# Attention and two expert layers: scores, exponentials and maxima in single PSUM banks, two of each, and four instead of seven of nine key tiles in full float32 in the first batch

## The chip, the cores and the metric

The kernel runs on one core of one Trainium2 chip. The metric is the device time of one execution in microseconds (us), here the median of three. Engines are named as in the profile: PE is TensorE (matmuls; PEld its weight loads), DVE is VectorE, ACT is ScalarE, POOL is GpSimd, SP is SyncE, which issues most of the DMAs.

## What is computed

Attention with pooled queries over 4 batches of 8 heads, then a dense layer of three products with a maximum, then a layer of 8 experts with one expert for each token. Only the first part is touched by the change.

```python
q_pool = q.reshape(B, H, S // factor, factor, D).mean(axis=3)     # 4, 8, 576, 64
scores = scale * np.matmul(q_pool, k.transpose(0, 1, 3, 2))       # 576 x 1152 a head
scores = scores - np.max(scores, axis=-1, keepdims=True)
attn = np.exp(scores)
attn = attn / (np.sum(attn, axis=-1, keepdims=True) + 1e-09)
x = np.matmul(attn, v)                                            # 576 x 64 a head
...
h = np.maximum(np.maximum(x @ w1, x @ w2), x @ w3)                # 2304 x 512 -> 768
x = h @ w_out                                                     # -> 512
...
e_idx = np.argmax(x @ w_gate, axis=1)                             # one of 8 experts
ye = np.maximum(x[mask] @ w1[e], 0.0) @ w2[e]                     # 512 -> 1024 -> 512
```

## The kernel before

**Stages.** The work of attention goes by pairs of heads: 16 pairs (p), four to a batch. A pair has 2 heads x 9 key tiles = 18 tiles (n counts them through, 288 in all). The dense layer runs in four groups, one for each batch, as filling between the steps of attention: group g is spread over the time of batch g+1, and the last group and the experts come after attention. Each engine executes its own queue in order, and the order of all queues is that in which the program emits its instructions: `attention()` (L455) yields after every step, and at each yield the main loop may emit some steps of the dense layer (`fill_step`, L1118; a step is three matmuls at L869 to L871). How many is set by `st["at"]`, the place of attention in tiles, and not by any time.

**A tile.** `sT` (L346) makes the scores of 128 keys against all 576 queries of a head in float32r: four matmuls of 288 columns (L353, L354) into one PSUM buffer of two banks, `s`. ScalarE takes the exponential of both banks in one instruction (L355) to `P`. In most tiles ScalarE then casts P to float16 (`ph`, L361), and in `rest` (L365) VectorE, or GpSimd for a few, makes the low half `pl` (L373). `av` (L376) sums the values with both halves (L398, L403): ten float16 matmuls. A tile for which `direct` (L342) holds has no halves: its weighted sum takes float32 matmuls on P (L389), ten in the trace. Before the change these are the key tiles 1 to 7 of each head in the first batch. The order of a slot n (L538 to L566) is: scores of tile n, planned work up to n + 0.25, `av` of tile n-2, planned work up to n + 0.5, `rest` of tile n-1, planned work up to n + 0.75.

**The roughs.** The maximum of each score row is taken from a product in one rounding, `rough` (L300), during the pair before. For each of 9 query tiles and each half of the keys there are two matmuls of 288 columns (L315) into one two-bank buffer and one maximum over both (L316): 18 steps a pair. The buffer is `g`, of which there is one; up to pair 4 it alternates with `r`, another pair of banks (in pair 0 also with `s`); after that `r` is closed and its banks become the two buffers `f` of the dense layer. `g` also serves the scaling of V (L215) and the transposes that end a pair (`fin4`, L435). A rough needs `bd`, a block diagonal of the queries that DMAs fill (L274).

**The planner.** `plan_pair` (L512) puts the preparation of pair p+1 on a list by due times in tiles: the roughs from 5.4 to 16.4 of the 18 tiles. `plan_conv` (L533) puts steps of `convert` (L596) there, which splits the dense layer's weights, given in 64 bits, into two float32 parts by six VectorE instructions a unit (L623 to L637), with a fetch and a store by DMA: 22 steps in each pair until the 26 units are done, in pair 7.

[...]

Of the kernel before, what the change touches and what calls it, by code (L numbers as in the profile page):

```python
# [27 lines left out]
def moe_attention(ctx, tc, q, k, v, wa, wb, w_gate, w_og, e_w1, e_w2, out):  # L28
# [4 lines left out]
    D = 64  # L33
# [28 lines left out]


    NCV = (22, 22)
# [17 lines left out]

    ps_r = ExitStack()
    st["ps_r"] = ps_r.enter_context(tc.tile_pool(name="ps_r", bufs=1, side="right", space=PSUM))
# [5 lines left out]
    ps_g = pa.enter_context(tc.tile_pool(name="ps_g", bufs=1, space=PSUM))  # L90
    ps_s = pa.enter_context(tc.tile_pool(name="ps_s", bufs=1, space=PSUM))
# [112 lines left out]
    def prep_v(p):  # L204
# [10 lines left out]
        ps = ps_g.tile([128, 2, 512], F32, name="g")  # L215
        nc.tensor.matmul(ps[:, 0, 0:128], ones, dg, start=True, stop=True)
        vx = pp.tile([128, 1], F32, name="vx", bufs=1)
        nc.vector.tensor_reduce(out=vx, in_=ps[:, 0, 0:128], axis=AX.X, op=ALU.max)
# [81 lines left out]
    def rough(p):  # L300
        rk = st[p, "rk"]
        mx2 = pp.tile([128, QT, 2], F32, name="mx2")
        for i in range(2 * QT):
            t, c = i // 2, i % 2

            x = i % 3 if p == 0 else i % 2 if p <= NP else 0
            if x == 0:
                ps = ps_g.tile([128, 2, 512], F32, name="g")
# [9 lines left out]
        if p == NP:  # L318
            ps_r.close()
            st["ps_f"] = pf.enter_context(tc.tile_pool(name="ps_f", bufs=2, side="right", space=PSUM))  # L320
        mx = pp.tile([128, QT], F32, name="mx")
        nc.vector.tensor_reduce(out=mx, in_=mx2, axis=AX.X, op=ALU.max)
# [17 lines left out]
        yield 0  # L340

    def direct(p, kt):  # L342

        return pairs[p][0] == 0 and 0 < kt < KT - 1

    def sT(p, h, kt):  # L346
        q1, q2 = st[p, "q1"], st[p, "q2"]
        P = pp.tile([128, 2, QC], F32, name="P", bufs=3)
        ps = ps_s.tile([128, 2, 512], F32, name="s")
        ks = slice(kt * 128, kt * 128 + 128)  # L350
        for c in range(2):
            cs = slice(c * QC, c * QC + QC)
            nc.tensor.matmul(ps[:, c, 0:QC], t1[h][:, ks], q1[h][:, cs], start=True, stop=False)  # L353
            nc.tensor.matmul(ps[:, c, 0:QC], t2[h][:, ks], q2[h][:, cs], start=False, stop=True)  # L354
        nc.scalar.activation(P, ps[:, :, 0:QC], AF.Exp, scale=0.5 / (D ** 0.5))  # L355
# [7 lines left out]
        yield 525  # L363
# [71 lines left out]
    def fin4(p):  # L435
        b, j = pairs[p]
        xa = st.pop((p, "xa"))
        o = (b * NQ) % RING
        ps = ps_g.tile([128, 2, 512], F32, name="g")
        for t in range(QA):  # L440

            c0 = min(t * 128, NQ - 128)
            c, d = (0, c0) if t < 3 else (1, c0 - 384)
            nc.tensor.transpose(ps[:, c, d:d + 128], xa[:, t], ident)
        n = [384, NQ - 384]
        for c in range(2):
            nc.scalar.copy(ring[:, 0, j, o + c * 384:o + c * 384 + n[c]], ps[:, c, 0:n[c]])
        yield 550
        for c in range(2):
            x = slice(o + c * 384, o + c * 384 + n[c])  # L450
            nc.vector.tensor_tensor(out=ring[:, 1, j, x], in0=ps[:, c, 0:n[c]], in1=f32(ring[:, 0, j, x]), op=ALU.subtract)
        st["fin"] = p
        yield 0

    def attention():  # L455
# [11 lines left out]
        for i in range(2 * QT):  # L467
# [44 lines left out]
        def plan_pair(p):  # L512
# [15 lines left out]
            at = sorted([t + 6 + x for x in range(11)] + [t + x + 0.4 for x in (5, 6, 8, 10, 12, 14, 16)])  # L528
            steps(rough(p), at + [t + 16.6, t + 16.7, t + 16.7])
# [9 lines left out]
        while n < len(tiles) + 2 or plan:  # L539
            if n < len(tiles):  # L540
# [30 lines left out]
    def psf():  # L571
        return st.get("psf", st["ps_f"]).tile([128, 512], F32, name="f")
# [99 lines left out]
    def ffn():  # L672
# [32 lines left out]
        def logits(lt, c0, nm, cs=range(NK)):  # L705

            if cs[0] == 0:
                st["pl"] = psf() if "psf" not in st else st["ps_f"].tile([128, 512], F32, name="f")
# [477 lines left out]
```

## Time and profile before

| | us |
|---|---|
| median of three runs | 1290.95 (1290.26 to 1293.16) |
| the profiled execution | 1294.97 |
| its span, first to last instruction | 1292.9 |
| PE busy | 1126.3 (87%), 8558 instructions |
| PE weight loads busy | 1006.4 (78%) |
| DVE busy | 836.9 (65%), 1380 instructions |
| ACT busy | 636.3 (49%), 1076 instructions |
| POOL busy | 320.2 (25%) |
| mean granted TensorE clock | 0.942 |

The first exponential starts at 30.1 us, pair 4 at 216.7, pair 8 at 445.5; the last exponential ends at 870.3. The shares are averages over stages with different limits, so the rows below are taken by stage. In a group of instructions the first number after the bar is the busy time of all, the second the mean duration in ns, and after the next bar stands the idle time of the engine just before them with what ended it. Matmuls overlap in the pipeline, and so do their rows.

### The profile page before, as it was taken

To read this page: it belongs to the slowest core of one execution; us is meant where nothing else is said; L and a number is where in the kernel's file an instruction comes from. 1 tells how busy PE (TensorE), PEld (TensorE's weight loads), DVE (VectorE), ACT (ScalarE), POOL (GpSimd) and SP (SyncE) were. 2 spreads that over 40 slices of the span, in tenths; PEclk is the share of its full clock that TensorE was granted. 3 is DMA by queue.
4 is the path that set the end of the run, shared out by engine and by line. 5 is a ranking of instruction groups with operands and counts; after the bars stand their busy time and mean duration, and the time that the engine had idled before them with its cause. 6 is when DMAs were issued, how large, how long until landed. Compare 5 with 4: busy or idle time off the path is not lost.

```text
span 1292.9 us, 21963 instructions
## 1 busy us (share of the span) xinstructions
PE 1126.3 (87%) x8558; PEld 1006.4 (78%) x8558; DVE 836.9 (65%) x1380; ACT 636.3 (49%) x1076; POOL 320.2 (25%) x266
## 2 busy tenths in 40 slices
PE   4989887887888899899999889999995999999494
PEld 3888787776777789788889778899994778887383
DVE  8867889789888774768776686842515652226444
ACT  3544556465556563665764656662414442214433
POOL 2321323232323320231230202100104331113422
PEclk9877899799999998999999999999997999999697
DMA  7655777564644554454465454427934632103440
GB/s 206 163 117 155 198 216 190 153 186 143 185 156 128 136 150 135 127 160 148 118 172 165 112 149 120 117 75 259 322 116 141 230 107 101 50 32 130 168 164 17
DMA packets 88781, 191.11 MB, mean 148 GB/s; under 512 B 32302, under 2 KB 42542, under 8 KB 88624
## 3 DMA queue, kind: packets, MB, share of 16 engines
q1 hardware_dynamic: 76320, 150.74, 35.9%
q10 hardware_dynamic: 7824, 28.91, 10.4%
q0 software_dynamic: 4480, 9.49, 2.3%
q8 instruction: 85, 1.39, 0.5%
q14 instruction: 72, 0.59, 0.1%
HBM read 134.32 MB, written 22.59 MB: 121 GB/s over the span
## 4 chain that ended last, share of the span: by engine, by line
PE 42%; DVE 20%; DMA 19%; issue 11%; ACT 4%; POOL 1%; ACTq 1%; POOLq 0%; SPq 0%; DVEq 0%
DMA yg<-y_dram,idx 11%; PE f L869 7%; DVE pl L373 6%; DVE mx L316 6%; PE f L870 6%; PE f L871 6%; PE g L315 5%; PE s L353 4%; PE s L354 4%; PE av L389 3%; PE av L398 3%; DMA out_dram<-o,idx 3%; PE av L403 2%; DMA bd<-q 2%; ACT P L355 2%
## 5 line engine op out<-in xcount | busy, mean ns | idle before, releaser
L355 ACT ACTIVATE P<-s 128x576 f32<-128x576 f32 x288 | 187.5, 651 | 293.9 <-PE s L354 284.1
L316 DVE TENSOR_REDUCE mx<-g 128x1 f32<-128x576 f32 x240 | 180.7, 753 | 89.8 <-PE g L315 89.3
L869 PE MATMUL f<-ring,wt 128*128 128x288 f32 x576 | 189.4, 329 | 12.5 <-DVE hm L882 5.8
L373 DVE TENSOR_TENSOR pl<-P,ph 128x576 f16<-128x576 f32 x212 | 182.6, 866 | 14.2 <-ACT ph L361 13.9
L353 PE MATMUL s<-q,t 128*128 128x288 f32 x576 | 177.5, 321 | 10.4 <-ACT P L355 9.2
L870 PE MATMUL f<-ring,wt 128*128 128x288 f32 x576 | 173.8, 302 | 0.0
L354 PE MATMUL s<-q,t 128*128 128x288 f32 x576 | 171.1, 310 | 2.3 <-DVE q L334 2.3
L871 PE MATMUL f<-ring,wt 128*128 128x288 f32 x576 | 173.0, 300 | 0.0
L315 PE MATMUL g<-rk,bd 128*128 128x288 f32 x480 | 123.4, 340 | 43.7 <-DVE mx L316 21.3
L361 ACT CAST ph<-P 128x576 f16<-128x576 f32 x232 | 156.0, 672 | 7.4
L398 PE MATMUL av<-vv,ph 128*128 128x129 f16 x1160 | 158.1, 226 | 0.3 <-ACT ev L410 0.3
L403 PE MATMUL av<-vv,pl 128*128 128x65 f16 x1160 | 119.2, 197 | 34.3 <-DVE pl L373 31.3
L315 PEld LDWEIGHTS g<-rk,bd 128*128 128x128 f32 x480 | 79.3, 202 | 66.4 <-DVE mx L316 41.7
L403 PEld LDWEIGHTS <-pl 128*128 128x128 f16 x1160 | 91.8, 100 | 47.5 <-DVE pl L373 46.7
L353 PEld LDWEIGHTS s<-q,t 128*128 128x128 f32 x576 | 115.3, 200 | 15.1 <-ACT P L355 13.4
L869 PEld LDWEIGHTS f<-ring,wt 128*128 128x128 f32 x576 | 111.9, 194 | 16.1 <-DVE hm L882 7.7
L354 PEld LDWEIGHTS s<-q,t 128*128 128x128 f32 x576 | 115.7, 201 | 4.9 <-DVE q L334 4.9
L870 PEld LDWEIGHTS f<-ring,wt 128*128 128x128 f32 x576 | 112.8, 196 | 0.0
L398 PEld LDWEIGHTS <-ph 128*128 128x128 f16 x1160 | 98.3, 99 | 17.8
L871 PEld LDWEIGHTS f<-ring,wt 128*128 128x128 f32 x576 | 112.1, 195 | 0.0
L425 POOL TENSOR_TENSOR ev<-ev 128x320 f32<-128x320 f32 x32 | 30.3, 947 | 322.1 <-ACT ev L410 322.1
L958 DVE TENSOR_TENSOR W<-raw,W 128x1024 fp32r<-128x1024 f32 x48 | 84.2, 1769 | 26.4 <-ACT W L952 21.5
(170 smaller groups left out, 2309.1 us busy)
## 6 DMA issues: line engine op xcount, KB each, us to landing
wt<-whl SPq DMA_DIRECT2D x72, 512.0 KB, 3.6
raw<-in_e_w_dram SPq DMA_DIRECT2D x64, 512.0 KB, 5.9
t<-rk ACTq DMA_DIRECT2D x64, 288.0 KB, 4.1
wt<-whl SPq DMA_DIRECT2D x32, 384.0 KB, 3.4
kf<-in_k_dram SPq DMA_DIRECT2D x16, 576.0 KB, 5.0
vf<-in_v_dram SPq DMA_DIRECT2D x16, 576.0 KB, 4.8
t<-lk ACTq DMA_DIRECT2D x32, 288.0 KB, 5.6
wd<-in_wa_dram SPq DMA_DIRECT2D x18, 512.0 KB, 5.7
```

Of the source, the lines that this page charges most:

```text
L315: nc.tensor.matmul(ps[:, x, 0:QC], bd[:, t, :], rk[:, k0:k0 + QC], start=True, stop=True)
L316: nc.vector.tensor_reduce(out=mx2[:, t, c:c + 1], in_=ps[:, :, 0:QC], axis=AX.XY, op=ALU.max)
L353: nc.tensor.matmul(ps[:, c, 0:QC], t1[h][:, ks], q1[h][:, cs], start=True, stop=False)
L354: nc.tensor.matmul(ps[:, c, 0:QC], t2[h][:, ks], q2[h][:, cs], start=False, stop=True)
L355: nc.scalar.activation(P, ps[:, :, 0:QC], AF.Exp, scale=0.5 / (D ** 0.5))
L361: nc.scalar.copy(ph, pv)
L373: eng.tensor_tensor(out=pl, in0=pv, in1=ph, op=ALU.subtract)
L398: nc.tensor.matmul(a[:, o:o + W1], ph[:, q0:q0 + 128], vt[:, kt, 0:W1], start=first and t % 3 == 0, stop=z,)
L403: nc.tensor.matmul(a[:, o + D:o + W1], pl[:, q0:q0 + 128], vt[:, kt, D:W1], start=False, stop=z)
L869: nc.tensor.matmul(ps[:, 0:G], hi[:, kk], xh, start=first, stop=False)
L870: nc.tensor.matmul(ps[:, 0:G], hi[:, kk], xl, start=False, stop=False)
L871: nc.tensor.matmul(ps[:, 0:G], lo[:, kk], xh, start=False, stop=last)
```

## The change

- The buffers `g` and `s` become two buffers of one bank each instead of one of two banks. `r` goes; from the start there are two one-bank buffers `f`, which the roughs share up to pair 4 with `g` in turn (in pair 0 also with `s`).
- A rough is one matmul of 384 columns and one maximum over them: 27 steps a pair in place of 18, over due times 5.5 to 16.4.
- The scores of a tile are made in two halves of 288 queries, each with its own bank, its own exponential and a yield behind it; planned work that is due runs between the halves.
- `rest` of tile n-1 is emitted right behind the scores of tile n, ahead of the planned work and of `av` of tile n-2.
- In the first batch the key tiles 1, 3, 5 and 7 of each head stay in full float32; 2, 4 and 6 are split like the others.
- 18 steps of conversion in each of pairs 0 to 3 and 25 in each later pair until done, in place of 22.
- `fin4` takes its transposes in two parts, one bank each, a quarter of a tile apart.

The diff, without what only follows from the new shapes:

```diff
-    NCV = (22, 22)
+    RW = (5.5, 16.4)
+    NCV = (18, 25)
...
-    st["ps_r"] = ps_r.enter_context(tc.tile_pool(name="ps_r", bufs=1, side="right", space=PSUM))
+    ps_f = pf.enter_context(tc.tile_pool(name="ps_f", bufs=2, side="right", space=PSUM))
...
-    ps_g = pa.enter_context(tc.tile_pool(name="ps_g", bufs=1, space=PSUM))
-    ps_s = pa.enter_context(tc.tile_pool(name="ps_s", bufs=1, space=PSUM))
+    ps_g = pa.enter_context(tc.tile_pool(name="ps_g", bufs=2, space=PSUM))
+    ps_s = pa.enter_context(tc.tile_pool(name="ps_s", bufs=2, space=PSUM))
...
     def rough(p):
         rk = st[p, "rk"]
-        mx2 = pp.tile([128, QT, 2], F32, name="mx2")
-        for i in range(2 * QT):
-            t, c = i // 2, i % 2
-
-            x = i % 3 if p == 0 else i % 2 if p <= NP else 0
-            if x == 0:
-                ps = ps_g.tile([128, 2, 512], F32, name="g")
-            elif x == 1:
-                ps = st["ps_r"].tile([128, 2, 512], F32, name="r")
-            else:
-                ps = ps_s.tile([128, 2, 512], F32, name="s")
-            for x in range(2):
-                k0 = c * NQ + x * QC
-                nc.tensor.matmul(ps[:, x, 0:QC], bd[:, t, :], rk[:, k0:k0 + QC], start=True, stop=True)
-            nc.vector.tensor_reduce(out=mx2[:, t, c:c + 1], in_=ps[:, :, 0:QC], axis=AX.XY, op=ALU.max)
-            yield 265
...
+        mx3 = pp.tile([128, QT, 3], F32, name="mx3")
+        banks = 0
+        for c in range(3):
+            for t in range(QT):
+
+                x = banks % (3 if p == 0 else 2) if p <= NP else 0
+                banks += 1
+                if x == 0:
+                    ps = ps_g.tile([128, 512], F32, name="g")
+                elif x == 1:
+                    ps = psf()
+                else:
+                    ps = ps_s.tile([128, 512], F32, name="s")
+                nc.tensor.matmul(ps[:, 0:384], bd[:, t, :], rk[:, c * 384:(c + 1) * 384], start=True, stop=True)
+                nc.vector.tensor_reduce(out=mx3[:, t, c:c + 1], in_=ps[:, 0:384], axis=AX.X, op=ALU.max)
+                yield 175
...
-        return pairs[p][0] == 0 and 0 < kt < KT - 1
+        return pairs[p][0] == 0 and kt % 2
...
         P = pp.tile([128, 2, QC], F32, name="P", bufs=3)
-        ps = ps_s.tile([128, 2, 512], F32, name="s")
         ks = slice(kt * 128, kt * 128 + 128)
         for c in range(2):
+            ps = ps_s.tile([128, 512], F32, name="s")
             cs = slice(c * QC, c * QC + QC)
...
-        nc.scalar.activation(P, ps[:, :, 0:QC], AF.Exp, scale=0.5 / (D ** 0.5))
...
+            nc.scalar.activation(P[:, c], ps[:, 0:QC], AF.Exp, scale=0.5 / (D ** 0.5))
+            if c == 0:
+                yield 262
...
-            at = sorted([t + 6 + x for x in range(11)] + [t + x + 0.4 for x in (5, 6, 8, 10, 12, 14, 16)])
-            steps(rough(p), at + [t + 16.6, t + 16.7, t + 16.7])
+            r0, r1 = RW
+            steps(rough(p), [t + r0 + (r1 - r0) * x / 26 for x in range(27)] + [t + r1 + x for x in (0.2, 0.3, 0.3)])
...
-                yield from sT(p, h, kt)
+                for j, x in enumerate(sT(p, h, kt)):
+                    st["at"] = n + 0.25 * j
+                    yield x
+                    yield from due(n + 0.25 * j)
+            if 0 <= n - 1 < len(tiles):
+                rest(*tiles[n - 1])
             yield from due(n + 0.25)
...
-                        steps(fin4(p), [n + FN[3], n + FN[3] + 0.8])
+                        for i, g in enumerate(QG):
+                            steps(fin4(p, *g), [n + FN[3] + 0.25 * i, n + FN[3] + 0.6 + 0.25 * i])
             yield from due(n + 0.5)
-            if 0 <= n - 1 < len(tiles):
-                rest(*tiles[n - 1])
```

## Rows read from the trace of the kernel before

**Rows 1.** Windows by stage (start:end us, length, busy us (instructions) by engine, granted clock, DMA)
```profile
30.10:216.70 186.60, 162.10 (x1159) 155.03 (x1159) 148.67 (x239) 92.06 (x153) 48.65 (x46) 0.85 0.63 171
216.70:445.50 228.80, 187.74 (x1631) 166.03 (x1631) 191.96 (x300) 131.82 (x228) 73.01 (x56) 0.94 0.53 157
332.10:392.70 60.60, 48.69 (x421) 42.94 (x419) 49.99 (x81) 34.15 (x60) 19.15 (x16) 0.94 0.52 158
392.70:445.50 52.80, 46.09 (x419) 41.55 (x420) 42.82 (x66) 31.52 (x55) 18.13 (x14) 0.97 0.46 129
445.50:870.30 424.80, 396.21 (x3685) 361.40 (x3683) 295.09 (x532) 259.60 (x458) 84.87 (x68) 0.99 0.47 135
```

**Rows 2.** Timeline of PE (start us, busy us, what): a float32 tile's sum, a split one's
```profile
135.67 1.22 PE L389 MATMUL av<-yT,P 128*128 128x65 f32 x10
136.73 0.72 PE L444 MATMUL g<-ident,xa 128*128 128x128 f32 x5
...
560.03 0.23 PE L398 MATMUL av<-vv,ph 128*128 128x129 f16 x1
...
560.46 0.38 PE L869 MATMUL f<-ring,wt 128*128 128x288 f32 x1
```

**Rows 3.** Single lines (duration ns min/median/max, first and last start, shapes)
```profile
L316 DVE TENSOR_REDUCE mx<-g x240: 717/757/760, 11.1 to 828.9; 128x1 f32<-128x576 f32 x120
L218 DVE TENSOR_REDUCE vx<-g x16: 284/292/293, 18.7 to 804.0; 128x1 f32<-128x128 f32 x16
L880 ACT COPY hm<-f x48: 392/399/416, 241.3 to 940.8; 128x288 f32<-128x288 f32 x48
```

**Rows 4.** Timeline in pair 6, idle time before in brackets
```profile
366.48 0.75 DVE L316 TENSOR_REDUCE mx<-g 128x1 f32<-128x576 f32 x1
...
367.29 0.54 PE L315 MATMUL g<-rk,bd 128*128 128x288 f32 x2 [1.43 <-DVE mx L316]
...
367.86 0.76 DVE L316 TENSOR_REDUCE mx<-g 128x1 f32<-128x576 f32 x1 [0.63 <-PE g L315]
```

**Rows 5.** Waits in pairs 4 to 7 (us in all, times, longest)
```profile
DVE mx L316 <- PE g L315: 22.1, 35, 2.0
PE av L403 <- DVE pl L373: 17.2, 22, 2.7
```

**Rows 6.** Waits in pairs 0 to 3
```profile
DVE mx L316 <- PE g L315: 18.3, 15, 3.1
DVE mx L316 <- PE r L315: 11.0, 14, 1.7
...
PE s L353 <- ACT P L355: 6.8, 12, 1.7
```

**Rows 7.** The page's group of exponentials
```profile
L355 ACT ACTIVATE P<-s 128x576 f32<-128x576 f32 x288 | 187.5, 651 | 293.9 <-PE s L354 284.1
```

**Rows 8.** Groups of DVE in pairs 0 to 3
```profile
L637 DVE SCALAR_TENSOR_TENSOR wo<-ce,ca 128x512 fp32r<-128x512 int32 x14 | 13.6, 970 | 0.2
...
L373 DVE TENSOR_TENSOR pl<-P,ph 128x576 f16<-128x576 f32 x15 | 12.2, 810 | 0.0
...
L635 DVE TENSOR_SCALAR ca<-wo 128x512 int32<-128x512 int32 x14 | 8.5, 607 | 0.3
```

**Rows 9.** Waits from pair 8 to the last exponential
```profile
PEld L403 <- DVE pl L373: 18.7, 50, 1.9
PEld g L315 <- DVE mx L316: 13.8, 51, 1.3
PE av L403 <- DVE pl L373: 9.9, 21, 1.7
...
PE g L315 <- DVE mx L316: 3.7, 6, 1.0
```

**Rows 10.** Timeline of PE and the window after it, in pair 1
```profile
90.59 0.82 PE L315 MATMUL g<-rk,bd 128*128 128x288 f32 x2 [3.68 <-DMA bd<-q]
...
88.50:102.20 13.70, 11.61 (x52) 11.64 (x53) 5.61 (x11) 2.95 (x5) 0.00 (x0) 0.50 0.35 120
```

More of the change, by code (lines that the diff above doesn't have):

```diff
@@ L214, in prep_v @@
         yield 0
-        ps = ps_g.tile([128, 2, 512], F32, name="g")
-        nc.tensor.matmul(ps[:, 0, 0:128], ones, dg, start=True, stop=True)
+        ps = ps_g.tile([128, 512], F32, name="g")
+        nc.tensor.matmul(ps[:, 0:128], ones, dg, start=True, stop=True)
         vx = pp.tile([128, 1], F32, name="vx", bufs=1)
-        nc.vector.tensor_reduce(out=vx, in_=ps[:, 0, 0:128], axis=AX.X, op=ALU.max)
+        nc.vector.tensor_reduce(out=vx, in_=ps[:, 0:128], axis=AX.X, op=ALU.max)
         yield 220
@@ L301, in rough @@
         rk = st[p, "rk"]
-        mx2 = pp.tile([128, QT, 2], F32, name="mx2")
-        for i in range(2 * QT):
-            t, c = i // 2, i % 2
-            x = i % 3 if p == 0 else i % 2 if p <= NP else 0
-            if x == 0:
-                ps = ps_g.tile([128, 2, 512], F32, name="g")
-            elif x == 1:
-                ps = st["ps_r"].tile([128, 2, 512], F32, name="r")
-            else:
-                ps = ps_s.tile([128, 2, 512], F32, name="s")
-            for x in range(2):
-                k0 = c * NQ + x * QC
-                nc.tensor.matmul(ps[:, x, 0:QC], bd[:, t, :], rk[:, k0:k0 + QC], start=True, stop=True)
-            nc.vector.tensor_reduce(out=mx2[:, t, c:c + 1], in_=ps[:, :, 0:QC], axis=AX.XY, op=ALU.max)
-            yield 265
-        if p == NP:
-            ps_r.close()
-            st["ps_f"] = pf.enter_context(tc.tile_pool(name="ps_f", bufs=2, side="right", space=PSUM))
+        mx3 = pp.tile([128, QT, 3], F32, name="mx3")
[5 more added lines that the diff above has]
+                if x == 0:
+                    ps = ps_g.tile([128, 512], F32, name="g")
+                elif x == 1:
[5 more added lines that the diff above has]
+                yield 175
         mx = pp.tile([128, QT], F32, name="mx")
-        nc.vector.tensor_reduce(out=mx, in_=mx2, axis=AX.X, op=ALU.max)
+        nc.vector.tensor_reduce(out=mx, in_=mx3, axis=AX.X, op=ALU.max)
         yield 0
@@ L348, in sT @@
         P = pp.tile([128, 2, QC], F32, name="P", bufs=3)
-        ps = ps_s.tile([128, 2, 512], F32, name="s")
         ks = slice(kt * 128, kt * 128 + 128)
         for c in range(2):
+            ps = ps_s.tile([128, 512], F32, name="s")
             cs = slice(c * QC, c * QC + QC)
-            nc.tensor.matmul(ps[:, c, 0:QC], t1[h][:, ks], q1[h][:, cs], start=True, stop=False)
-            nc.tensor.matmul(ps[:, c, 0:QC], t2[h][:, ks], q2[h][:, cs], start=False, stop=True)
-        nc.scalar.activation(P, ps[:, :, 0:QC], AF.Exp, scale=0.5 / (D ** 0.5))
+            nc.tensor.matmul(ps[:, 0:QC], t1[h][:, ks], q1[h][:, cs], start=True, stop=False)
+            nc.tensor.matmul(ps[:, 0:QC], t2[h][:, ks], q2[h][:, cs], start=False, stop=True)
+            nc.scalar.activation(P[:, c], ps[:, 0:QC], AF.Exp, scale=0.5 / (D ** 0.5))
+            if c == 0:
+                yield 262
         pv = P.rearrange("p c n -> p (c n)")
@@ L362, in sT @@
         st[p, h, "P", kt] = (pv, ph)
-        yield 525
+        yield 262
     def rest(p, h, kt):
@@ L433, in fin3, with fin4 @@
         )
-    def fin4(p):
+    QG = ((0, (0, 1, 2)), (384, (3, 4)))
+    def fin4(p, c0, tiles):
         b, j = pairs[p]
[L437 to L452, printed above, removed]
+        xa = st[p, "xa"]
+        o = (b * NQ) % RING + c0
+        n = min(384, NQ - c0)
+        ps = ps_g.tile([128, 512], F32, name="g")
+        for t in tiles:
+            q0 = min(t * 128, NQ - 128) - c0
+            nc.tensor.transpose(ps[:, q0:q0 + 128], xa[:, t], ident)
+        c = slice(o, o + n)
+        nc.scalar.copy(ring[:, 0, j, c], ps[:, 0:n])
+        yield 330
+        nc.vector.tensor_tensor(out=ring[:, 1, j, c], in0=ps[:, 0:n], in1=f32(ring[:, 0, j, c]), op=ALU.subtract)
+        if c0:
+            st["fin"] = p
         yield 0
@@ L466, in attention @@
         ro, pv = rough(0), prep_v(0)
-        for i in range(2 * QT):
+        for i in range(3 * QT):
             yield next(ro)
@@ L571, in psf @@
     def psf():
-        return st.get("psf", st["ps_f"]).tile([128, 512], F32, name="f")
+        return st.get("psf", ps_f).tile([128, 512], F32, name="f")
     chunks = []
@@ L707, in logits @@
             if cs[0] == 0:
-                st["pl"] = psf() if "psf" not in st else st["ps_f"].tile([128, 512], F32, name="f")
+                st["pl"] = psf() if "psf" not in st else ps_f.tile([128, 512], F32, name="f")
             pl = st["pl"]
```

1 line of the change is left out of this document (removed).

## Prediction

> **What bounds the kernel now.** I read the stages first, then the waits inside each, then single instructions. The windows cut the span at the first exponential and at every fourth pair [rows 1]. The reader is to see that the limit moves. In pairs 0 to 3 (30.1 to 216.7 us) TensorE and VectorE are both busy for most of the time, 162.1 and 148.7 us of 186.6, and TensorE has a granted clock of 0.85 only. In pairs 4 to 7 (228.8 us) VectorE leads, 192.0 us. That it sets the pace there is shown by two neighbours: pair 6, with 22 conversion steps, has 50.0 us of VectorE work and lasts 60.6 us; pair 7, with hardly any left, has 42.8 us and lasts 52.8. So 7.2 us less work came back as 7.8 us less time. From pair 8 on (445.5 to 870.3) TensorE is busy 396.2 of 424.8 us and VectorE 295.1: TensorE sets the end. After 870.3 nothing of the change runs but the last pair's end.
>
> A busy TensorE is not a full one here: the row of ten matmuls in [rows 2] shows 1.22 us, but the next kind starts 1.06 us after it, so rows overlap. I price TensorE's work by start-to-start times and its stalls by waits.
>
> **The change part by part.**
>
> *Roughs (the maxima).* 18 reduces of 576 columns a pair become 27 of 384; the columns stay 1152 for each query tile. A reduce takes 757 ns at 576 and 292 at 128 columns [rows 3]; a straight line gives 0.56 us at 384 (an estimate from these two). So 27 x 0.56 = 15.0 us stand against 18 x 0.757 = 13.6: VectorE gets 1.4 us more a pair, in all 16. Bounds: 0.7 (if half of the 0.16 us that the line leaves for zero columns is covered by the instruction before) and 1.4; I take 1.4. The first pair's roughs run before the first exponential, with only preparation beside them: +1.4 us. TensorE has 9 weight loads a pair fewer and the same columns, about nothing.
>
> [...]
>
> *Two banks in place of one pair.* The stall that it removes stands in the trace as a ping-pong [rows 4]: VectorE reduces from 366.48 to 367.23; only then may the next rough matmuls write the one buffer, so TensorE, which had waited 1.43 us, starts them at 367.29; VectorE then waits 0.63 us for them. With two banks the second is written while the first is read. In pairs 4 to 7 VectorE waits 22.1 us (35 times) for such matmuls [rows 5]. In pairs 0 to 3 it waits 18.3 + 11.0 us [rows 6], though the old code had two buffers there already.
>
> *Exponentials in halves.* 288 of 651 ns [rows 7] become 576. The nearest row is ScalarE's copy of 128x288 out of PSUM, 399 ns [rows 3]: two are 0.80 us, 0.15 more a tile, 43 us in all. ScalarE is busy 92.1 of 186.6, 131.8 of 228.8 and 259.6 of 424.8 us [rows 1], and its wait before an exponential is mostly for the scores, so I cost this at nothing; without that cover it would be 0.15 x 18 = 2.7 us a pair. TensorE's wait for the score buffer (6.8 us in pairs 0 to 3 [rows 6]) should go, but VectorE is late next there, so I count no gain for it.
>
> *Three more of nine tiles split in the first batch.* 3 x 8 heads = 24 tiles. TensorE: ten full float32 matmuls start at 135.67 and the next kind at 136.73, 1.06 us; a split tile goes from 560.03 to 560.46, 0.43 us [rows 2]. So 24 x 0.63 = 15 us fewer, 18 at the granted 0.85. VectorE: 24 subtractions of 0.81 us [rows 8] = 19.4 us more. ScalarE: 24 casts, not the bound.
>
> *Conversion.* 88 steps in pairs 0 to 3 become 72; 16 move behind pair 4, with their share of fetches and stores on SP's queue. The six VectorE lines of a unit run from 970 to 607 ns (the dearest and the cheapest of six [rows 8]), mean 0.78: 12.5 us move from pairs 0 to 3 into pairs 4 to 7.
>
> *The low half earlier.* The subtraction for tile n-1 is put ahead of the planned work and of the weighted sum of tile n-2 instead of behind both. It waits for a ScalarE cast issued one tile before; behind it in VectorE's queue now stand the roughs of that slot, and if the cast were late they would wait too. For it: TensorE waits for this subtraction 17.2 us in pairs 4 to 7 [rows 5] and at least 9.9 us after [rows 9].
>
> *The transposes in two banks.* Same copies and subtractions, 0.05 of a tile later: nothing.
>
> **The sum by stage**, on the profiled execution (1292.9 us of span, 1294.97 in all, which is 4.0 above the median 1290.95):
> - before the first exponential: +1.4.
> - pairs 0 to 3: VectorE +19.4 + 4 x 1.4 - 12.5 = +12.5 us. Against it its waits for rough matmuls (29.3 us) shrink by what leaves TensorE's queue ahead of them, 18 us: -5.5. Bounds: no wait goes, +12.5; all go, -16.8.
> - pairs 4 to 7: VectorE +5.6 + 12.5 = +18.1. Its waits for rough matmuls were 22.1; the longest, 2.0, I leave out, since a pair's first rough matmul also waits for the DMA of bd (as in [rows 10]); the other 20.1 go: -2. Bounds: +18 (they only move) and -18 (all of VectorE's 36.8 idle us go).
> - pairs 8 to 15: TensorE's stalls on this subtraction and on the reduces are 9.9 + 3.7 us by the matmuls' own gaps and 18.7 + 13.8 by the weight loads' [rows 9]. The first leaves out what a running matmul covers, the second counts some covered time; the middle is 23. I charge the whole extra VectorE work of seven pairs, 9.8: -13. Bounds: -32 and +10.
>
> Sum: 1.4 - 5.5 - 2 - 13 = -19, so 1294.97 becomes 1276, and beside the median 1290.95 - 19 = 1272 us.
>
> **The rivals.**
>
> 1. *VectorE becomes the bound and no wait goes.* Place: pairs 0 to 7, where it is busy 340.6 of 415.4 us. The change adds 12.5 + 18.1 = 30.6 us; the 74.8 idle us stay if they come from the order of the queues (a reduce stands right behind its own matmul, whatever the buffer) and not from the buffer. It decides from the point at which less than 19 us of the 74.8 vanish. Price: +1.4 + 30.6 - 13 = +19, 1310 us. For it: the first batch had two buffers already and still waits 29.3 us. Against: the 0.63 us pattern of [rows 4] is the buffer's. Between this and the forecast lie times of 1294 to 1310. Chance 0.17.
>
> 2. *Waits only change their name.* TensorE no longer waits for the subtraction but for the reduce behind it: the last stage gives 0 and the others cancel, 1288 to 1293 us. For it: VectorE is busy about 70% in the last stage, and its order of work stays. Chance 0.08.
>
> 3. *The clock.* [...] Chance 0.12.
>
> 4. *More gain.* From pair 8 on the weight loads' figure goes (32 us) against half of the added VectorE work (5 us): -27. Pairs 0 to 3 come near their bound, -14, and pairs 4 to 7 lose half of what is left of VectorE's idle time, -8. With +1.4 that is -48, 1243 us. For it: the pattern of [rows 4] repeats. Against: all of it would have to come off the path. Chance 0.08.
>
> 5. *The change does not do what it says*: the halves' score banks gain nothing because TensorE reaches the scores late anyway. I count no gain for them, so the forecast holds.
>
> **How the numbers follow.** The forecast case (1254 to 1284) has 0.55, and the rivals 0.17, 0.08, 0.12 and 0.08. Predicted 1272 us. The range leaves out the upper part of rival 1 and most of rival 4, about 2 in 10: 1250 to 1297. About 0.2% is what a measurement of this kernel can tell from no change, 1288.4 to 1293.5. Faster: 0.55 + 0.12 + 0.08 = 0.75; the same: rival 2 without the part beside it, 0.07; slower: rival 1 and that part, 0.18.
>
> **What would show it.** Right: VectorE's waits for rough matmuls in pairs 4 to 7 fall from 22 us to under 6; reduces of about 0.56 us; exponentials of about 0.4 us twice; the stage from pair 8 is some 13 us shorter with TensorE's waits for the subtraction under 8 us; pairs 0 to 3 are a little shorter with VectorE over 87% busy. Wrong: reduces over 0.6 us; pairs 4 to 7 over 235 us; a granted clock under 0.8 in pairs 0 to 3; TensorE's waits there moved to the reduces.

## The result and the profile after

The changed kernel takes 1247.4 us (median of 4 runs, 1243.9 to 1254.3) against 1292.06 before: ratio 0.966, 95% interval 0.960 to 0.971. Timed once more beside other kernels it gave 1246.2 us, ratio 0.959 (0.956 to 0.963). Executions of one kernel differ (`b4`: 1276 to 1307 us, at a mean granted clock of 0.956 to 0.923); ratios compare the faster ones, and the profiles of two slower ones (`b4` at 1299 us, `c1` at 1256) are not compared by stage. The prediction was 19 us less; 45 us less were measured, and 1247 us lies just below the range (1250 to 1297).

The profiled execution (1254.3 us, span 1252.3) by stage, with the same columns as [rows 1]: start:end, length, busy us of PE, PEld, DVE, ACT and POOL, granted clock, DMA. The stages are pairs 0 to 3, 4 to 7, 8 to 15, and what follows.

```profile
31.80:205.20 173.40, 146.76 (x1125) 136.62 (x1124) 158.97 (x283) 112.12 (x246) 49.16 (x47) 0.87 0.61 165
205.20:419.80 214.60, 177.87 (x1600) 161.29 (x1599) 200.72 (x352) 140.49 (x303) 75.61 (x57) 0.95 0.62 181
419.80:822.70 402.90, 378.08 (x3612) 355.78 (x3613) 302.30 (x595) 275.13 (x602) 87.06 (x67) 0.99 0.50 143
822.70:1252.30 429.60, 369.23 (x2054) 314.44 (x2050) 176.08 (x276) 144.12 (x227) 107.64 (x80) 0.92 0.41 138
```

Against [rows 1] the stages are 13.2, 14.2 and 21.9 us shorter. The stretch before the first exponential is 1.7 us longer (30.1 to 31.8), and the last one 7.0 us longer, although next to nothing of the change runs there; over all kernels of this study it took 417 to 430 us. In this profile TensorE waits 14.4 us in all in front of the experts' first product, in those where the stretch is shorter than 423 us 8.9 to 12.2; why is not known. In the first two stages VectorE is now idle for 14.4 and 13.9 us only, where it was 37.9 and 36.8.

The waits that [rows 5] and [rows 9] show, after the change: first pairs 4 to 7 (us in all, times, longest), then pairs 8 to 15.

```profile
DVE mx L315 <- PE g L314: 5.7, 10, 1.6
...
PE av L401 <- DVE pl L371: 15.0, 12, 2.5
```
```profile
PEld g L314 <- DVE mx L315: 10.0, 16, 1.3
...
PE g L314 <- DVE mx L315: 6.0, 10, 1.1
...
PEld L401 <- DVE pl L371: 4.1, 6, 1.5
...
PE av L401 <- DVE pl L371: 3.2, 5, 1.3
```

VectorE's wait for rough matmuls fell from 22.1 to 5.7 us. From pair 8 on, TensorE's weight loads wait 14.1 us for reduces and low halves in place of 32.5; the gaps of the matmuls themselves fell from 13.6 to 9.2 only. Line numbers differ from kernel to kernel: `mx` is always the reduce, `pl` the low half. The new instructions cost what was estimated: a reduce 547 ns (estimate 560), an exponential of half a tile 410 (estimate 399).

```profile
L315 DVE TENSOR_REDUCE mx<-g x362: 517/547/560, 10.9 to 782.3; 128x1 f32<-128x384 f32 x181
```
```profile
L351 ACT ACTIVATE P<-s x576: 387/410/448, 31.8 to 822.3; 128x288 f32<-128x288 f32 x192
```

The ping-pong of [rows 4] has become rare. In pairs 4 to 7, 53 of the 108 rough matmuls into `g` run for 0.05 us or more while a reduce reads the other buffer; before the change none of 144 does. In pair 6 two reduces stand one behind the other without a gap (two in 1.01 us), so the second bank was full before the first was read to its end:

```profile
346.52 1.01 DVE L315 TENSOR_REDUCE mx<-g 128x1 f32<-128x384 f32 x2
347.56 0.81 DVE L264 TENSOR_TENSOR q<-qf,q 64x576 fp32r<-64x576 f32 x1
```

### The profile page after: what moved, and what is told of

The parts are those of the page before. It is cut to its first block, busy times and chain, and to the rows that moved or that the text cites. A ratio compares the mean times of both kernels' runs of the same rounds, so it can differ in the third digit from the quotient of the medians.

```text
span 1252.3 us, 22102 instructions
## 1 busy us (share of the span) xinstructions
PE 1084.7 (87%) x8414; PEld 977.5 (78%) x8414; DVE 861.8 (69%) x1548; ACT 680.5 (54%) x1388; POOL 325.9 (26%) x266
## 5 line engine op out<-in xcount | busy, mean ns | idle before, releaser
L351 ACT ACTIVATE P<-s 128x288 f32<-128x288 f32 x576 | 223.9, 410 | 217.0 <-PE s L350 194.6
L315 DVE TENSOR_REDUCE mx<-g 128x1 f32<-128x384 f32 x362 | 194.5, 548 | 40.1 <-PE g L314 37.7
L371 DVE TENSOR_TENSOR pl<-P,ph 128x576 f16<-128x576 f32 x236 | 203.7, 865 | 22.9 <-ACT ph L359 17.9
L349 PE MATMUL s<-q,t 128*128 128x288 f32 x576 | 183.1, 321 | 9.8 <-ACT P L351 8.9
L350 PE MATMUL s<-q,t 128*128 128x288 f32 x576 | 176.2, 309 | 7.2 <-DVE q L330 7.2
L359 ACT CAST ph<-P 128x576 f16<-128x576 f32 x256 | 172.1, 672 | 8.1
L314 PE MATMUL g<-rk,bd 128*128 128x384 f32 x362 | 139.0, 390 | 38.6 <-DVE mx L315 22.4
L396 PE MATMUL av<-vv,ph 128*128 128x129 f16 x1280 | 168.2, 228 | 0.2 <-ACT ev L408 0.2
L401 PE MATMUL av<-vv,pl 128*128 128x65 f16 x1280 | 132.6, 198 | 32.2 <-DVE pl L371 31.9
L401 PEld LDWEIGHTS <-pl 128*128 128x128 f16 x1280 | 106.4, 101 | 37.8 <-DVE pl L371 37.3
L349 PEld LDWEIGHTS s<-q,t 128*128 128x128 f32 x576 | 116.1, 202 | 14.9 <-ACT P L351 13.4
L396 PEld LDWEIGHTS <-ph 128*128 128x128 f16 x1280 | 107.7, 100 | 23.2 <-issue 1.1
```

The costliest lines, as they stand in the source:

```text
L314: nc.tensor.matmul(ps[:, 0:384], bd[:, t, :], rk[:, c * 384:(c + 1) * 384], start=True, stop=True)
L315: nc.vector.tensor_reduce(out=mx3[:, t, c:c + 1], in_=ps[:, 0:384], axis=AX.X, op=ALU.max)
L349: nc.tensor.matmul(ps[:, 0:QC], t1[h][:, ks], q1[h][:, cs], start=True, stop=False)
L350: nc.tensor.matmul(ps[:, 0:QC], t2[h][:, ks], q2[h][:, cs], start=False, stop=True)
L351: nc.scalar.activation(P[:, c], ps[:, 0:QC], AF.Exp, scale=0.5 / (D ** 0.5))
L359: nc.scalar.copy(ph, pv)
```

## The experiments

The table has all timed kernels: the ratio to the kernel before with its 95% interval, then the lengths of the stages in the one profiled execution of each. A single profile of pairs 0 to 3 is uncertain by some 8 us: the changed kernel showed 173.4 and 171.6 us, and one that differs only from pair 8 on (`c3`) 165.4. The stage from pair 8 on repeats within 3 us. Dashes: stages not compared.

| kernel | ratio | interval | 0 to 3 | 4 to 7 | 8 to 15 |
|---|---|---|---|---|---|
| before | 1 | | 186.6 | 228.8 | 424.8 |
| changed | 0.966 | 0.960, 0.971 | 173.4 | 214.6 | 402.9 |
| changed, again (`e3`) | 0.959 | 0.956, 0.963 | 171.6 | 213.9 | 400.1 |
| changed, low half late (`a1`) | 0.980 | 0.971, 0.989 | 175.7 | 221.4 | 408.5 |
| changed, roughs as before (`a4`) | 0.983 | 0.976, 0.989 | 173.6 | 225.6 | 416.2 |
| changed, scores as before (`a5`) | 0.971 | 0.967, 0.975 | 168.3 | 218.5 | 409.3 |
| changed, seven float32 tiles (`a2`) | 0.973 | 0.967, 0.980 | 167.5 | 213.9 | 400.2 |
| changed, 22 conversion steps (`a3`) | 0.965 | 0.959, 0.971 | 175.7 | 203.8 | 401.8 |
| changed, both of the last two (`c1`) | 0.958 | 0.953, 0.963 | - | - | - |
| the same again (`e2`) | 0.962 | 0.957, 0.966 | 187.9 | 204.0 | 400.7 |
| before + banks for roughs (`b3`) | 0.984 | 0.977, 0.991 | 186.2 | 213.7 | 414.3 |
| before + early low half (`b1`) | 0.998 | 0.994, 1.002 | 188.2 | 217.8 | 421.2 |
| before + both (`e1`) | 0.970 | 0.966, 0.974 | 184.2 | 204.7 | 412.2 |
| before + halves of scores (`b4`) | 0.995 | 0.992, 0.999 | - | - | - |
| before + four float32 tiles (`b2`) | 1.000 | 0.997, 1.003 | 184.4 | 225.6 | 425.5 |
| changed, more VectorE work from pair 8 (`c3`) | 0.971 | 0.967, 0.975 | 165.4 | 211.9 | 417.6 |
| changed, 22 and 14 conversion steps (`d1`) | 0.962 | 0.958, 0.965 | 176.2 | 194.6 | 415.2 |
| changed, more on GpSimd (`f2`) | 0.968 | 0.961, 0.975 | 175.8 | 209.3 | 401.0 |
| changed, one buffer for roughs (`f3`) | 1.028 | 1.022, 1.034 | 180.2 | 243.9 | 442.8 |

### One part undone at a time

`a1`, the low half late:

```diff
-            if 0 <= n - 1 < len(tiles):
-                rest(*tiles[n - 1])
             yield from due(n + 0.25)
...
             yield from due(n + 0.5)
+            if 0 <= n - 1 < len(tiles):
+                rest(*tiles[n - 1])
```

> The changed kernel with one part undone: the low half of tile n-1 is emitted again behind the weighted sum of tile n-2 and the planned work. Theory A (the place in VectorE's queue carries the gain from pair 8 on): that stage, 402.9 us in the changed kernel, goes back to about 420, TensorE's wait for the low half there rises from under 6 to over 15 us, and the whole is 1262 to 1275 us. Theory B (the banks carry the gain): the stage stays under 409 us and the whole under 1255.

1267 us: the whole as theory A had it, but not for its reason. From pair 8 on the stage went to 408.5 only, so the early low half is 6 to 8 us there and not 18, and the weight loads' wait for it rose to 7.2 us, not to over 15; 7 us more are in pairs 4 to 7.

`a4`, the roughs, their buffers and the transposes as before, except that pair 0 takes turns between `g` and `r` alone, since `s` keeps its two single banks:

```diff
-    ps_f = pf.enter_context(tc.tile_pool(name="ps_f", bufs=2, side="right", space=PSUM))
+    st["ps_r"] = ps_r.enter_context(tc.tile_pool(name="ps_r", bufs=1, side="right", space=PSUM))
...
-    ps_g = pa.enter_context(tc.tile_pool(name="ps_g", bufs=2, space=PSUM))
+    ps_g = pa.enter_context(tc.tile_pool(name="ps_g", bufs=1, space=PSUM))
...
-                nc.tensor.matmul(ps[:, 0:384], bd[:, t, :], rk[:, c * 384:(c + 1) * 384], start=True, stop=True)
-                nc.vector.tensor_reduce(out=mx3[:, t, c:c + 1], in_=ps[:, 0:384], axis=AX.X, op=ALU.max)
+            nc.vector.tensor_reduce(out=mx2[:, t, c:c + 1], in_=ps[:, :, 0:QC], axis=AX.XY, op=ALU.max)
```

> The changed kernel with the roughs, their buffers and the transposes as before (18 steps of two banks, one buffer from pair 5 on; in pair 0 two buffers instead of three); halves of scores, the early low half, four float32 tiles and the conversion steps stay changed. Theory A: VectorE's waits for rough matmuls in pairs 4 to 7 come back (5.7 to 18 us or more) and with them 10 to 18 us there, while the stage from pair 8 on stays within 6 us of 402.9: 1256 to 1270 in all. Theory B (the banks carry the gain from pair 8 on too): that stage goes back over 415 us, 1270 to 1285 in all.

1269 us. The stage from pair 8 on went back to 416.2, over theory B's line, though the whole stayed in theory A's range; in pairs 4 to 7 VectorE's waits for rough matmuls came back to 11.7 us and the stage to 225.6. So the banks carry more from pair 8 on than the early low half, and each of the two, undone, costs some 20 us of the 45.

`a2` and `a3`, the four tiles and the conversion steps:

```diff
-        return pairs[p][0] == 0 and kt % 2
+        return pairs[p][0] == 0 and 0 < kt < KT - 1
```
```diff
-    NCV = (18, 25)
+    NCV = (22, 22)
```

> The changed kernel with seven of nine key tiles in full float32 in the first batch, as before. Theory A (TensorE's lighter work is what shortened pairs 0 to 3, VectorE's added 20 us are beside it): pairs 0 to 3 go from 173.4 to 182 us or more, the whole to 1254 to 1262. Theory B (VectorE sets the pace there, the three tiles cost it 20 us and the banks alone gave the gain): pairs 0 to 3 fall to 165 us or less and the whole to 1236 to 1242.

> The changed kernel with 22 conversion steps in each pair, as before, so that 16 steps (about 12 us of VectorE) move back into pairs 0 to 3. If VectorE sets the pace in both stages: pairs 0 to 3 about 185, pairs 4 to 7 about 203 us, the whole within 4 us of 1247. If only pairs 4 to 7 are set by it: pairs 0 to 3 stay at 175 and the whole falls to 1236 to 1240.

`a2`: five runs from 1234 to 1260 us, the profiled one the fastest; the ratio in the table rests on three of them, 1251 to 1260. Its pairs 0 to 3 (167.5) lie near theory B's 165, and its time decides nothing. `a3`: 1245 us. 16 steps fewer made pairs 4 to 7 10.8 us shorter for 10.7 us of VectorE work, so VectorE sets the pace there; pairs 0 to 3 became 2 to 4 us longer for 7.6 us more of its work, which is within the 8 us of a single profile.

`a5`, scores in one buffer of two banks, one exponential, no planned work between the halves:

```diff
-    ps_s = pa.enter_context(tc.tile_pool(name="ps_s", bufs=2, space=PSUM))
+    ps_s = pa.enter_context(tc.tile_pool(name="ps_s", bufs=1, space=PSUM))
...
-            nc.scalar.activation(P[:, c], ps[:, 0:QC], AF.Exp, scale=0.5 / (D ** 0.5))
-            if c == 0:
-                yield 262
+        nc.scalar.activation(P, ps[:, :, 0:QC], AF.Exp, scale=0.5 / (D ** 0.5))
```

> The changed kernel with the scores of a tile in one buffer of two banks again and one exponential over both (and no planned work between the halves); single-bank roughs, early low half, four float32 tiles and the conversion steps stay changed. Theory H (in the first batch TensorE stood at the one score buffer, and the halves took that away): pairs 0 to 3 go from 173.4 to 182 us or more, the whole to 1256 to 1270. Theory N (the prediction's: nothing, VectorE is late next): every stage within 4 us, 1243 to 1252 in all.

1256 us. Pairs 0 to 3 are not longer (168.3), so theory H falls; but theory N falls too: the stage from pair 8 on is 6 to 9 us longer than with halves. The weight loads there wait 13.4 us for reduces (29 times), with halves 10.0 (16 times).

### One part alone

These three start from the kernel before. `b3` makes the edit of `a4` the other way round, `b4` that of `a5` (its roughs in pair 0 take turns between `g` and `r` alone), and `b1` that of `a1`:

```diff
+            if 0 <= n - 1 < len(tiles):
+                rest(*tiles[n - 1])
             yield from due(n + 0.25)
```

> The kernel before with the roughs alone changed: single banks, two of each, 27 steps of 384 columns, the transposes in two parts. Undone in the changed kernel this part cost about 21 us. If the parts add up: 1266 to 1276. If the banks only help once the low half is early (the queue's order holds the reduces back else): 1280 to 1293. If VectorE's added 1.4 us a pair decides in pairs 0 to 7 when it stands alone: over 1293.

> The kernel before with the low half of tile n-1 alone moved ahead of the planned work and of the weighted sum of tile n-2. Undone in the changed kernel it cost about 15 to 20 us. If the parts add up: 1270 to 1280. If its wait only changes its name while the roughs have one buffer: 1287 to 1293, with TensorE's waits for the reduces up by what those for the low half go down.

> The kernel before with the scores alone changed: halves in two single banks, an exponential for each, planned work between them (pair 0's roughs in two buffers instead of three). Theory H: pairs 0 to 3 fall from 186.6 to 178 us or less, 1278 to 1286 in all. Theory N: within 4 us of 1292. If ScalarE's added time (about 0.15 us a tile, 43 us in all) shows: over 1296.

The banks alone: 1271 us, 20 us less, all from pair 4 on. The early low half alone: no difference (ratio 0.998). Halves of scores alone: 0.5% less, 6 us, although they give ScalarE more work. 20 + 2 + 6 us are 28 of the 45. The profile of the early low half alone is at odds with its median: at 1287.2 us it is 7 us faster, and its pairs 4 to 7 are 11.0 us shorter than before the change. What happens to the waits is seen in the weight loads from pair 8 on: first with the early low half alone, then with the banks alone.

```profile
PEld g L315 <- DVE mx L316: 18.4, 58, 1.4
...
PEld L403 <- DVE pl L373: 4.5, 6, 1.9
```
```profile
PEld L400 <- DVE pl L370: 21.0, 41, 1.9
...
PEld g L315 <- DVE mx L316: 5.1, 17, 0.6
```

Before, they were 13.8 for the reduces and 18.7 for the low half [rows 9]. Each part removes most of its own wait and the other one grows: 13.8 to 18.4, and 18.7 to 21.0. So some of the wait changes its name, as the prediction's second rival has it: 4.6 of the 14.2 us that the early low half takes away, 2.3 of the 8.7 that the banks take. The rest is gone: 9.6 and 6.4 us.

### Two parts together

`e1` is `b3` with the edit of `b1`.

> The kernel before with two parts alone: single-bank roughs and the early low half. Alone they gave 20 and 2 us. Theory S (each part only renames TensorE's wait while the other's cause stays, so the pair gives more than its sum): 1250 to 1262 us, with TensorE's waits from pair 8 on for the low half and for the reduces both under half of the kernel before (18.7 and 13.8 us by its weight loads). If they add up and the rest of the gain lies with the halves and the tiles: 1268 to 1276.

1259 us, ratio 0.970: 40 us less than before, where the singles add up to 22 (by the ratios the surplus is 16 us, give or take 12, and the two sets ran on different chips). Theory S holds for the time. Of its waits one part held: the low half's fell to 4.6 us, the reduces' stayed at 13.4 in 29 waits instead of 51; together 18.0 in place of 32.5.

```profile
PEld g L315 <- DVE mx L316: 13.4, 29, 1.4
...
PEld L400 <- DVE pl L370: 4.6, 6, 1.9
```

But the profiles show no surplus. These waits fell by 14.5 us, alone by 9.6 + 6.4 = 16.0. Pairs 4 to 7 are 24.1 us shorter than before, alone 11.0 + 15.1; from pair 8 on 12.6, alone 3.6 + 10.5; the profiled executions are 35 us faster than that of the kernel before, alone 8 + 30. The profiles of the singles are 7 and 6 us faster than their medians, that of the two together is not. The early low half undone in the changed kernel (`a1`) costs 15 us over the three stages and gives 13 alone. So the reason that theory S gives, more than the sum because each part only renames the wait, is not borne out, and the surplus in the medians stays unexplained.

From pair 8 on the gaps in front of matmuls are not the whole stall: from before the change to after, TensorE's idle time fell by 3.8 us and its busy time by 18.1, for the same columns at the same granted clock of 0.99. An estimate from the start of each matmul to the start of the next, less what the same pair of kinds takes unstalled in these traces, gives the stall in front of roughs and low halves: 41 us before, 31 with the early low half alone, 30 with the banks alone, 19 with both, 16 in the changed kernel. By this too the parts add up. It also settles a rival: fewer weight loads gained nothing, for from its start to the next matmul's an unstalled rough matmul takes 0.132 us of 288 columns and 0.176 of 384, by the traces of the two kernels: 36 and 27 of them are 4.75 us a pair both before and after.

### The first batch

`b2` is the kernel before with four float32 tiles (the edit of `a2` the other way round); `c1` and `e2` are the changed kernel with the edits of `a2` and `a3` together; `e3` is the changed kernel once more, on the chip of `e2`.

> The kernel before with four instead of seven of nine key tiles in full float32 in the first batch, nothing else. It takes some 15 us of TensorE's work away there and gives VectorE 19 us. Theory W: pairs 0 to 3 fall from 186.6 to 180 us or less, 1284 or less in all. Theory Q: they stay or grow by up to 8 us, 1290 to 1300 in all.

> The changed kernel with two parts undone together: seven of nine key tiles in full float32 in the first batch, and 22 conversion steps in each pair; so single-bank roughs, halves and the early low half are all that is changed. Theory Q (these three, which act on the queues, carry the whole gain; the four tiles and the conversion steps only move work): 1240 to 1250 us, pairs 0 to 3 within 5 us of the changed kernel's 173.4. Theory W (the lighter work of TensorE in the first batch is what shortened pairs 0 to 3): these go back to 181 to 188 us while pairs 4 to 7 fall to about 204.

> Once more the changed kernel with seven float32 tiles and 22 conversion steps a pair, for an undisturbed profile. If the first batch needs the four tiles: pairs 0 to 3 at 181 to 188 us. If not: 165 to 178, and the whole at or under the changed kernel's.

> The changed kernel itself, unaltered, beside the two others on the same chip: 1244 to 1252 us; its second profile tells how far pairs 0 to 3 (173.4 us in the first) differ between executions of one kernel.

Four float32 tiles alone: ratio 1.000, pairs 0 to 3 at 184.4. Without the four tiles and the moved steps, the changed kernel's time is the same (0.962 beside 0.959 on one chip; 0.958 in the earlier set), but its stages are not: pairs 0 to 3 as theory W had them, 187.9, and pairs 4 to 7 10 us shorter. Beside `e3`, `e2` is 16.3 us longer in the first stage, 9.9 shorter in the second and 9.2 shorter behind attention (419.7 us; 419.1 in `a2`, but 428.9 and 429.6 in the changed kernel's two profiles). So in these profiles what the two parts gain in the first batch is paid back in the next stage and behind attention; that they cause the latter is not shown.

The wait that the forecast for this stage rested on does depend on the tiles. VectorE's waits for rough matmuls, 29.3 us before, are 16.9 with the four tiles alone and 9.8 and 7.5 in the changed kernel's two profiles, but 22.8 in `a2` and 29.8 in `e2`. First the changed kernel, then `a2`, then `e2`:

```profile
DVE mx L315 <- PE g L314: 7.9, 6, 2.5
...
DVE mx L315 <- PE f L314: 1.8, 5, 0.6
```
```profile
DVE mx L315 <- PE g L314: 18.3, 10, 4.5
...
DVE mx L315 <- PE f L314: 4.5, 5, 1.9
```
```profile
DVE mx L315 <- PE g L314: 22.2, 12, 6.4
...
DVE mx L315 <- PE f L314: 7.6, 9, 1.7
```

In `a2` VectorE also has 19.5 us less work than in the changed kernel, so its stage is no longer for it. First the first stage of `e2`, then of `a2`, which differs by 16 conversion steps:

```profile
31.60:219.50 187.90, 162.15 (x1121) 155.88 (x1121) 151.11 (x276) 98.17 (x226) 48.78 (x47) 0.84 0.62 170
```
```profile
31.70:199.20 167.50, 149.20 (x1129) 141.36 (x1128) 139.47 (x259) 95.88 (x222) 50.21 (x47) 0.92 0.64 171
```

Of the 20 us between them 11.6 are VectorE's work and 8.8 its idle time, and the granted clock is 0.84 against 0.92. With four tiles a clock of 0.84 went with 171.6 us (`e3`). Whether the clock makes the difference with seven is not settled, and a single profile of this stage tells little.

### The price of VectorE's work where TensorE sets the pace

`c3` adds nine reduces of 384 columns out of SBUF in each pair from 8 to 14:

```diff
+                if p > 2 * NP and t % 3 == 0:
+                    more = pp.tile([128, 1], F32, name="more")
+                    nc.vector.tensor_reduce(out=more, in_=f32(rk[:, 0:384]), axis=AX.X, op=ALU.max)
```

> The changed kernel with nine more VectorE reduces of 384 columns out of SBUF in each pair from 8 to 14, spread between the roughs, about 0.5 us each: some 30 us more of VectorE's work in the stage that TensorE sets, and nothing else. If that work stands on the path (the prediction charged all of the change's added VectorE time there): 20 to 30 us more, 1268 to 1278. If TensorE hides it: under 8 us more, 1247 to 1255.

```profile
409.10:826.70 417.60, 381.99 (x3612) 356.31 (x3613) 329.11 (x658) 276.38 (x602) 85.60 (x67) 0.99 0.49 138
```

63 more of 0.54 us are 34 us; VectorE's busy time grew by 27 and the stage by 15 to 17 us, the median by 10. The truth lies between the two theories: of this work a part of 0.3 to 0.5 stands on the path. `d1`, below, gives another price for other work.

### One buffer or small steps

```diff
-    ps_g = pa.enter_context(tc.tile_pool(name="ps_g", bufs=2, space=PSUM))
+    ps_g = pa.enter_context(tc.tile_pool(name="ps_g", bufs=1, space=PSUM))
...
-                            steps(fin4(p, *g), [n + FN[3] + 0.25 * i, n + FN[3] + 0.6 + 0.25 * i])
+                            steps(fin4(p, *g), [n + FN[3] + 0.55 * i, n + FN[3] + 0.5 + 0.55 * i])
```

The second edit keeps the two parts of the transposes from overlapping: they share the one buffer, and without it (`f1`) the program deadlocks and there is no time.

> The changed kernel with one single-bank buffer for the roughs (and for V's scaling and the transposes, whose two parts follow one another instead of overlapping) instead of two; the 27 small steps and all else stay. If the second buffer is what the roughs gained by: VectorE's waits for rough matmuls in pairs 4 to 7 go from under 7 back to 20 us or more, and with 27 round trips a pair the whole to 1270 to 1300. If the smaller steps are: within 8 us of 1247.

1329 us, 82 more than with two: over the expectation's upper end, and slower than the kernel before. In pairs 4 to 7 the waits are these:

```profile
PEld g L314 <- DVE mx L315: 40.7, 65, 2.1
...
DVE mx L315 <- PE g L314: 28.3, 49, 1.5
PE g L314 <- DVE mx L315: 25.4, 42, 1.9
```

VectorE waits 28.3 us (49 times) for rough matmuls instead of 5.7 (10 times); before the change it was 22.1 (35 times). So the second buffer is what the roughs gained by, not the small steps. Some of the 82 us may belong to V's scaling and the transposes, which also had two buffers; how much was not measured.

### Two versions meant to be better

> The changed kernel with 22 conversion steps in each of pairs 0 to 3 and 14 in each later one, so that about 13 steps (10 us of VectorE) leave pairs 0 to 7 and run in pair 8, where TensorE sets the pace. If VectorE sets the pace in pairs 4 to 7 and not from pair 8 on: pairs 4 to 7 about 195 us, the whole 1234 to 1242, better than both kernels. If the dense layer is held up for want of converted weights: over 1250.

> The changed kernel with more of the low halves on GpSimd in the first two batches: 3 of 10 a pair in the first (none before), 6 of 18 in the second (4 or 5 before); 12 and some 6 subtractions of 0.86 us leave VectorE in these stages. If VectorE sets the pace in both: pairs 0 to 3 about 164, pairs 4 to 7 about 209 us, the whole 1232 to 1240. If TensorE then waits for GpSimd's slower subtraction (1.3 us): over 1250.

`d1` (`NCV = (22, 14)`): 1247 us, no better. Pairs 4 to 7 are 20 us shorter, as expected, but with the 13 steps in pair 8 the stage from there on is 12 to 15 us longer. That is more than the 10 us of VectorE's work in them, where `c3` had 0.3 to 0.5 of the work; why was not tested. `f2` moves low halves to GpSimd:

```diff
-        eng = nc.gpsimd if b == 1 and (h * KT + kt) % 4 == 1 else nc.vector
+        eng = nc.gpsimd if b <= 1 and (h * KT + kt) % (4 - b) == 1 else nc.vector
```

1244 us, no better (the ratio in the table rests on the three fastest of 11 runs of the kernel before; their median, 1300, would give 0.957). In pairs 0 to 3 VectorE lost 11 of its 39 subtractions in the trace, and is busy as long as before (159.9 and 159.4 us), for others of its instructions were longer there. First the groups of the changed kernel's second profile, then of `f2`:

```profile
L371 DVE TENSOR_TENSOR pl<-P,ph 128x576 f16<-128x576 f32 x39 | 33.9, 870 | 3.4 <-ACT ph L359 3.4
...
L633 DVE SCALAR_TENSOR_TENSOR wo<-wd,ca 128x512 int32<-128x512 int32 x12 | 15.2, 1266 | 0.1
```
```profile
L371 DVE TENSOR_TENSOR pl<-P,ph 128x576 f16<-128x576 f32 x28 | 26.5, 947 | 3.4 <-ACT ph L359 3.4
L633 DVE SCALAR_TENSOR_TENSOR wo<-wd,ca 128x512 int32<-128x512 int32 x12 | 20.1, 1679 | 0.1
```

Which ones are longer can be read from single instructions. In the changed kernel's first profile the 32 of its 39 subtractions in pairs 0 to 3 that meet no GpSimd instruction take 735 to 759 ns; the 7 that overlap one take 831 to 1759.

## Why the prediction was wrong

Its direction, its stages and the two mechanisms of its largest terms were right; the size was 26 us too small. By its own steps:

- **Before the first exponential**: +1.4 forecast, +1.7 measured. **Behind the last one**: nothing forecast, +7.0 measured, unexplained.
- **Pairs 0 to 3**: -5.5 forecast, -13.2 and -15.0 measured, inside the bounds. VectorE got 10.3 us more (12.5 forecast), its waits for rough matmuls fell by 19.5 (18 forecast) and its other idle time by 4 (not counted). The mechanism stated, TensorE's lighter work ahead of the roughs, is borne out for the wait: it is 22.8 and 29.8 us with seven tiles in the changed kernel. What the tiles are worth in time is not settled: with seven the stage took 167.5 and 187.9 us, and the four tiles alone left 184.4.
- **Pairs 4 to 7**: -2 forecast, -14.2 measured. VectorE's idle time fell by 22.9 us, 20 were forecast. The term that was mis-sized is its work, +18.1 forecast and +8.8 measured. The moved conversion steps cost what they should (`a3`: 10.7 us of VectorE work, 10.8 us of time), and the reduces a little less than forecast. For the rest, the same instructions ran shorter than before: the low half of the dense layer's h (12 of 982 ns before, of 652 after, 4.0 us) and that of the tiles (53 of 958 and of 917, 2.2 us). The first is shown by its 12 instructions in this stage (minimum, median, maximum in ns), before and after:

```profile
L689 DVE TENSOR_TENSOR h<-hm,h x12: 443/795/1677, 269.2 to 440.5; 128x288 fp32r<-128x288 f32 x12
```
```profile
L691 DVE TENSOR_TENSOR h<-hm,h x12: 441/447/1690, 255.1 to 414.7; 128x288 fp32r<-128x288 f32 x12
```

Those that meet no GpSimd instruction take 441 to 460 ns in both kernels, 6 of 12 before and 8 after; the others take 1512 ns in the mean before, 1064 after. So the mean fell as fewer of them met GpSimd, and those for less. No part of the change aimed at that.

- **Pairs 8 to 15**: -13 forecast, -21.9 and -24.7 measured. Two terms failed. The whole of VectorE's added work, 9.8 us, was charged to the path; by `c3`, whose extra work is the same kind of reduce, 0.3 to 0.5 of it belongs there, 3 to 5 us. And the halves of scores were set at nothing, because "VectorE is late next there", an argument from the first batch that was carried over to a stage that VectorE does not set: `a5` and the step from `e1` to `e2` put them at 6 to 12 us there, in a stage where the weight loads' wait for the score buffer is at most 4.3 us in any profile. The weight loads' wait for reduces is about 3 us shorter with them; by which piece of the part (the earlier exponential, the planned work between the halves) is not settled.
- **The waits named for the last stage** were the right ones. Their size was not well read: of the matmuls' gaps (13.6 us) 4.4 went and of the weight loads' waits (32.5) 18.4, 11 in the middle where 23 were forecast. By start-to-start times the stall fell by some 25 us, so that 23 comes out near is partly luck.

Of the rivals, the first (VectorE the bound, no wait goes) failed: 23 idle us went from each of its two stages, 46 of 74.8 against its line of 19; its bound is nevertheless where pairs 4 to 7 now are. The second (waits change their name) is true in part, for a third or less of what each part alone takes away, and false for the whole. The third, the clock, did not come: 0.87 and 0.84 granted in the first batch, 0.85 before; what a clock under 0.8 there would have cost, for which its chance of 0.12 stands in the sum of the chances, no run shows. The fourth, more gain, came nearest, at 1243 us by its sum, with 0.08 for its chance, but not by its steps: it had all 32 us of the weight loads' waits go from pair 8 on, where 18.4 went and the halves gave the rest, and 8 us in pairs 4 to 7, where 14.2 came.

The choice was between the work that smaller steps add and the waits that a second bank takes away. With two banks in turn the kernel is 82 us faster than with one small bank (`f3`). The smaller steps have their price in the trace too, 27 x 0.547 against 18 x 0.757 us of reduces a pair, 1.1 us, and it is the smaller one.

## What to carry to other kernels

Two waits of one engine on another's queue can stand for each other in part: here 4.6 of the 14.2 us of wait that the early low half took away came back under the reduce's name (`b1`). When the times of two parts seem to give more than their sum (here 40 us for 20 + 2), look for the surplus in the stages and waits of the profiles before you explain it; here it is not there. Work added to an engine that does not set the pace of a stage need not be charged in full, but its share is not a constant: extra reduces between the roughs cost 0.3 to 0.5 of their time (`c3`), and with 10 us of conversion steps crowded into one pair the stage grew by 12 to 15 (`d1`). Look at single instructions before you carry a mean over: here VectorE's subtraction of the dense layer's low half took 0.44 to 0.46 us alone and up to 1.7 us where a GpSimd instruction ran beside it (pairs 4 to 7, both kernels), while the roughs' reduces took the same with one beside them (mean 0.544 us) as without (0.548). And smaller steps were worth it here only with the second buffer: 1247 us with two, 1329 with one, 1292 before the change.

## What was not expected

- One small buffer instead of two cost 82 us, 6.5%, in a kernel whose TensorE shows as busy for 87% of the span.
- Eleven subtractions given to GpSimd took nothing off VectorE's busy time in pairs 0 to 3 (159.9 us beside 159.4): one 512-column conversion instruction of VectorE went from 1266 to 1679 ns and its subtraction from 870 to 947.
- With seven float32 tiles in the first batch the granted clock of one stage was 0.84 and 0.92 in two kernels that differ by 16 conversion steps, and the stage 187.9 and 167.5 us.
